# Output projection of the first block by seven products between attention pieces, with its operand sums made in parts

## The chip, the cores and the metric

The kernel runs on one core of one Trainium2 chip. The metric is the device time of one execution in microseconds (us), the median of three runs. In the profile the engines are called PE (matmuls), PEld (the weight loads of PE), DVE (vector engine), ACT (scalar engine), POOL and SP (the last two mainly issue transfers here). "Tile" names such as hT, wO or xT are those of the program's buffers.

## The reference, cut to what matters

Attention whose keys and values are first projected from 1024 positions to 64, then a gated feed-forward layer:

```python
k_proj = einsum('ks,bhsd->bhkd', E, k); v_proj = einsum('ks,bhsd->bhkd', F, v)
attn   = softmax(q @ k_proj.T / 8)                 # 8 batches, 8 heads, 1024 x 64
x      = (attn @ v_proj) as [8192 tokens, 512]
gate   = 1 / (1 + exp(-(x @ w_gate)))              # w_gate, w_val: 512 x 1536
val    = x @ w_val
out    = (gate * val) @ w_out                      # w_out: 1536 x 512
```

The kernel handles the tokens in 16 blocks of 512, two for each batch. For most of the matrix products it uses a scheme with seven products of half-sized operands in place of eight (the operands are split 2 by 2, and sums of the parts, called S for the left and T for the right operand, take part in the products). Before the change the first block is the exception: its gate, its values and its output projection are plain products.

## The kernel before

Each engine runs its instructions in the order in which the program adds them. The first stage (attention of batch 0, block 0, block 1, and attention of batch 1) is ordered by hand: a list `todo` of slots, and for each slot functions that are put behind it. The rest is ordered by a small list scheduler, `arranged`.

```python
todo.append(lambda: first_pair(0, lambda: xo(1)))          # slot 0: hidden parts m = 0, 1
for m in range(2, NF):                                      # slots 1..10: m = 2..11
    todo.append(lambda m=m: mstep(0, m))
put(3, lambda: (qt2(0, ("DVE", "ACT")), qt2(1, ("DVE", "ACT"))))
put(4, lambda: (sc2(0), sc2(1)))
put(4, second_loads)
put(6, lambda: (den2(), xo2(0), xo2(1)))
put(7, lambda: (vt_sums(3, 0), vt_sums(2, 0)))              # DVE, 0.42 us each
put(8, lambda: bc2(0)())                                    # PE, then 2 DVE multiplications into xT
put(9, lambda: bc2(1)())                                    # the same for the other half of xT
put(10, x_sums(1, 1, 2)); put(10, lambda: vt_sums(1, 0))
# ... slots 11..38: block 1, three rounds of nine: gate steps and seven value products
def on(u, j, fn): put(11 + 9 * u + j, fn)
on(3, 0, n1["mixed"])                                       # slot 38
on(3, 0, lambda: [late1(x, g) for x in ("A0", "A1") for g in range(2)])
on(3, 0, h_sums(1, Z, 1, 2, 3))                             # DVE sums of block 1's hidden part
for tt in range(4):                                         # slots 39..42
    todo.append(lambda tt=tt: oproj(0, tt, FF.take()))
on(3, 1, n1["outputs"])
on(3, 2, lambda: n1["bc"](0))
on(3, 3, lambda: n1["bc"](1))
```

A step of the gated layer of block 0 makes two banks (gate and value, 4 matmuls of 512 columns each) and joins them; the DVE instruction of `gate` frees the value bank. There are four such banks.

```python
def mstep(blk, m):
    pbs = {n: ffn.next() for n in "GV"}
    for n in "GV":
        for i in range(NI):
            mm_one(blk, m, i, n, pbs[n])        # reads xT[:, i, block], all four i
    gate(blk, m, pbs["G"], pbs["V"])            # ACT tanh, DVE (tanh + 1) * value -> hT
```

The output projection of block 0, four times 12 matmuls of 512 columns, each with one DVE instruction that halves the sum on its way out of the bank:

```python
def oproj(blk, tt, pb, cols=((0, DM),)):
    ...
    for m in range(NF):
        mm(pb, bank[pb][:, 0 : c1 - c0], hT[blk % 2][:, m, tt * P : (tt + 1) * P], wO[:, m, c0:c1], ...)
    dve(lambda e: e.tensor_scalar(o[:, c0:c1], bank[pb][:, 0 : c1 - c0], 0.5, None, op0=ALU.mult), ...)
    FF.append(pb)
    add("SP", lambda e: e.dma_start(out_v[blk // 2, t][:, c0:c1], o[:, c0:c1]), ...)
```

The attention pieces of batch 1 that stand between them (`mixed`, `outputs`, `bc`). The banks FF (four) and AA (four) are handed on in the order in which the program gives them back:

```python
def mixed3():                                   # slot 38
    f, a0, a1 = FF.two(), AA.two(), AA.two()
    sc_one(3, f); xo_one(0, a0); xo_one(1, a1)  # PE
    for g in range(2): exp_half(3, g, f); FF.append(f[g])      # ACT
    later("A0", x_half, 0, a0, AA); later("A1", x_half, 1, a1, AA)   # ACT copies, give the banks back
def outputs3():                                 # slot 39
    f, a0 = FF.two(), AA.two()
    bd = AA.take()                              # the third AA bank to come back
    den8(bd); xo_one(2, f); xo_one(3, a0)       # PE: 16, 4 and 4 matmuls
    for g in range(2): x_half(2, g, f); ...     # ACT copies
    for g in range(2): x_half(3, g, a0); ...
    rec(0); rec(1)                              # DVE reciprocals of the denominators
    split()                                     # DVE: rden -> rhi, rhl (two instructions)
def bc(rnd):                                    # 8 matmuls that read rhl, into all four AA banks,
    ...                                         # then 4 DVE multiplications into xT
```

The sums of w_out (`t_sums`, four DVE instructions of 1536 elements a row) and of the weights of the gate (`gt_sums`, likewise) are made at the start of the scheduled stage; the former overwrite the place where bsel8, rhi and rhl lie:

```python
plan.tasks = []
...
next_kv, t_sums (3, 2), gt_sums (3, 2, 4, 1), xs_sums, t_sums (4, 1)
o_chain(1, ...)       # seven products for block 1's output projection
...
for t in arranged(tasks, {"DVE": 1.5}):         # when DVE is taken to be free, us after the stage's start
    ...
```

The weights of gate and value come in pieces of 256 columns, in the order of `m`:

```python
load_w(0, 0); load_w(0, 1); load_w(1); load_w(2)
for R in range(2): load_q_half(0, 1, R)
load_w(3); load_w(4); load_w(5)
```

Of the kernel before, what the change touches and what calls it, by code (L numbers as in the profile page):

```python
# [7 lines left out]
ALU = mybir.AluOpType  # L8
# [229 lines left out]
def bass_linformer_attn__then__ffn_glu_sigmoid_kernel(  # L238
# [18 lines left out]
    with contextlib.ExitStack() as es:  # L257
# [30 lines left out]
        identf = within([P, P], FP32)  # L288
        bsel8f = within([P, 4, 2, 64], FP32)
        early[0], used[0] = wT[:, :, :, :].rearrange("p a b c -> p (a b c)"), 0  # L290
        bsel8 = within([P, 4, 2, 64], BF16)
        kp = within([P, NR, DH], BF16)
        rhi = within([P, 256], BF16)
        rhl = within([P, 256], BF16)
        early[0], used[0] = gT[:, :, :, :].rearrange("p a b c -> p (a b c)"), 0
        rden = within([P, 256], FP32)
        rows = within([P, 4, 32], FP32)
# [93 lines left out]
        def dve(fn, r, w, b=None, t=None):  # L391
            x = [] if b is None else [("bank", b)]
            return add("DVE", fn, r=r, w=w, x=x, t=t)
# [78 lines left out]
        def start_loads():  # L472
            for src, rows, n in ((E, slice(0, 64), "E"), (F, slice(64, 128), "F")):
                add(
                    "SP",
                    lambda e, src=src, rows=rows: e.dma_start(EF[rows, :], src[:, :]),
                    w=[("EF", n)],
                    dma="in" + n,
                )
            for i in range(4):  # L480
                pool(
                    lambda e, i=i: e.memset(quad[32 * i : 32 * i + 32, :], 32.0 * i),  # L482
                    w=[("quad", i)],
                )
            for R in range(2):
                load_kv_heads(0, k, R)
                load_q_half(0, 0, R)
            for R in range(2):
                load_kv_heads(1, v, R)
            load_w(0, 0)  # L490
            load_w(0, 1)
            load_w(1)
            load_w(2)
            for R in range(2):
                load_q_half(0, 1, R)
            load_w(3)
            load_w(4)
            load_w(5)

        def heads8():  # L500
# [781 lines left out]
        def mm_one(blk, m, i, n, pb):  # L1282
# [8 lines left out]
                stop=(i == NI - 1),  # L1291
            )

        def gate(blk, m, pg, pv):
            M = blk * NF + m
            sg = sig[M % 3]
            act(
                sg, bank[pg][:, :], [], [("sig", M % 3, 0)], b=pg, func=AF.Tanh, scale=0.5
            )
            dve(  # L1300
                lambda e: e.scalar_tensor_tensor(
                    hT[blk % 2][:, m, :],
                    sg,
                    1.0,
                    bank[pv][:, :],
                    ALU.add,
                    ALU.mult,
                ),
                [("sig", M % 3, 0)],
                [("hT", blk % 2, m, n) for n in range(2)],  # L1310
                b=pv,
            )

        def oproj(blk, tt, pb, cols=((0, DM),)):
            o = vsnap[tt][:, :] if tt < 2 else ost[:, tt, :]
            ok = [("vsnap", tt)] if tt < 2 else None
            t = 2 * (2 * (blk % 2) + tt % 2) + tt // 2
            for n, (c0, c1) in enumerate(cols):
                if n:
                    pb = FF.take()  # L1320
                for m in range(NF):
                    mm(
                        pb,
                        bank[pb][:, 0 : c1 - c0],
                        hT[blk % 2][:, m, tt * P : (tt + 1) * P],
                        wO[:, m, c0:c1],
                        [("hT", blk % 2, m, tt // 2)] + (["wO0", "wO12"] if m < H6 else ["wO1"]),
                        start=(m == 0),
                        stop=(m == NF - 1),
                    )  # L1330
                dve(
                    lambda e, pb=pb, c0=c0, c1=c1: e.tensor_scalar(
                        o[:, c0:c1], bank[pb][:, 0 : c1 - c0], 0.5, None, op0=ALU.mult
                    ),
                    [],
                    ok or [("ost", tt, x) for x in ((0, 1) if len(cols) == 1 else (n,))],
                    b=pb,
                )
                FF.append(pb)
                add(  # L1340
                    "SP",
                    lambda e, c0=c0, c1=c1: e.dma_start(out_v[blk // 2, t][:, c0:c1], o[:, c0:c1]),
                    r=ok or [("ost", tt, x) for x in ((0, 1) if len(cols) == 1 else (n,))],
                    dma=f"out{tt}" if n == 0 else "outlast",
                )

        H6 = NF // 2

        def t_sums(n):
            B11, B12 = wO[:, 0:H6, 0:256], wO[:, 0:H6, 256:512]
            B21, B22 = wO[:, H6:NF, 0:256], wO[:, H6:NF, 256:512]
            T4, T3, T2 = [wT[:, i, :, :] for i in range(3)]
            o, a, b, op, r, w = {
                3: (T3, B22, B12, ALU.subtract, ["wO1", "wO12"], [("wT", 3)]),
                2: (T2, T3, B11, ALU.add, ["wO0", ("wT", 3)], [("wT", 2)]),
                4: (T4, B21, T2, ALU.subtract, ["wO1", ("wT", 2)], [("wT", 4)]),  # L1360
                1: (B12, B12, B11, ALU.subtract, ["wO0"], ["wO12", ("wT", 1)]),
            }[n]
            if n == 4:
                w = w + ["bsel8", ("kp", 0), ("kp", 1)]
                w += [(k, R) for k in ("rhi", "rhl") for R in range(2)]
            dve(lambda e: e.tensor_tensor(o, a, b, op), r, w, t=0.95)

        def s_sums(blk, n, ms, eng="DVE"):
            h, (m0, m1) = hT[blk % 2], ms
            lo, hi, up = slice(m0, m1), slice(H6 + m0, H6 + m1), range(m0, m1)  # L1370
            A11, A21 = h[:, lo, 0:256], h[:, lo, 256:512]
            A12, A22 = h[:, hi, 0:256], h[:, hi, 256:512]
            S1, S2 = hS[:, 0, lo, :], hS[:, 1, lo, :]
            o, a, b, op, r, w = {
                1: (S1, A21, A22, ALU.add, "A21 A22", "S1"),
                2: (S2, S1, A11, ALU.subtract, "S1 A11", "S2"),
                3: (A21, A11, A21, ALU.subtract, "A11 A21", "A21"),
                4: (A12, A12, S2, ALU.subtract, "A12 S2", "A12"),
            }[n]
            add(  # L1380
                eng,
                lambda e: e.tensor_tensor(o, a, b, op),  # L1382
                r=[k for x in r.split() for k in part(blk, x, up)],
                w=part(blk, w, up),
                t=0.95 if m1 - m0 == 6 else 0.6,
            )

        def part(blk, x, up):
            if x[0] == "S":
                return [(x, m) for m in up]  # L1390
            return [("hT", blk % 2, m + H6 * (x[2] == "2"), int(x[1]) - 1) for m in up]

        def product(blk, bk, A, B, start=False, stop=False, js=(0, 1), ms=(0, NF // 2), also=()):
            h = hT[blk % 2]
            for j in js:
                for m in range(*ms):
                    if A[0] == "S":
                        lhsT = hS[:, int(A[1]) - 1, m, j * P : (j + 1) * P]
                    else:
                        c = 256 * (A[1] == "2") + j * P  # L1400
                        lhsT = h[:, m + H6 * (A[2] == "2"), c : c + P]
# [61 lines left out]
        def evac(bk, tok, col):  # L1463
            o, keys = quarter(tok, col)
            act(o, bank[bk][:, :].rearrange("p (j c) -> p j c", j=2), [], keys, b=bk, scale=0.5)

        def o_chain(blk, a, c, goal, step, sums=True):
            turn = [0]
# [123 lines left out]
        def gt_sums(n, part=None):  # L1592
# [14 lines left out]
            w = [("gT", n, j) for j in js]  # L1607
            if n != 1:
                w += ["rows", "ident"] + [("rden", c, R) for c in range(2) for R in range(2)]
            if n == 1:  # L1610
                r, w = [("wG", j, 0) for j in js], w + [("wG", 3 + j, 0) for j in js]
            if n == 2:
# [324 lines left out]

        A, Z = (0, 4), (4, 6)
        todo.append(lambda: first_pair(0, lambda: xo(1)))
        for m in range(2, NF):  # L1940
            todo.append(lambda m=m: mstep(0, m))
        qt2, sc2, den2, bc2, xo2 = half_unit(1, att)
        put(3, lambda: (qt2(0, ("DVE", "ACT")), qt2(1, ("DVE", "ACT"))))
# [36 lines left out]
        def on(u, j, fn):  # L1980
            put(11 + 9 * u + j, fn)
# [21 lines left out]
        on(2, 0, h_sums(1, A, 1))  # L2003
        on(2, 4, h_sums(1, A, 2, 3))
        on(3, 0, h_sums(1, Z, 1, 2, 3))
        for tt in range(4):
            todo.append(lambda tt=tt: oproj(0, tt, FF.take()))
        on(3, 1, n1["outputs"])
        on(3, 2, lambda: n1["bc"](0))
        on(3, 3, lambda: n1["bc"](1))  # L2010

        for i, slot in enumerate(todo):
            slot()
# [19 lines left out]
            vd_one(XA, 0, b % 2)  # L2033
            vd_one(XA, 1, b % 2, b > 3)

        for n in (3, 2):
            t_sums(n)
        for n in (3, 2, 4):
            gt_sums(n)
        gt_sums(1)  # L2040
# [1 line left out]
            xs_sums(2, n)  # L2042
        next_kv(2, -2.0)
        transpose_q(["kpB"])
        t_sums(4)
        t_sums(1)
        o_chain(1, OA, OC, 0.0, 2.0, sums=False)
        for n in (1, 2, 3, 4):
            xs_sums(3, n)
# [43 lines left out]
                    xs_sums(2 * b + 3, i)  # L2093

        tasks, plan.tasks = plan.tasks, None
        for t in arranged(tasks, {"DVE": 1.5}):
            for eng, fn, r, w, x, dma in t.calls:
                add(eng, fn, r=r, w=w, x=x, dma=dma)

# [28 lines left out]
```

The softmax here doesn't subtract the row's maximum and nothing guards it: scores larger than these inputs give would overflow.

## Time and profile before

| | |
|---|---|
| median of 3 runs | 517.51 us (516.99 to 517.76) |
| span of the profiled execution | 515.9 us |
| PE busy | 505.0 us (98%) |
| DVE busy | 410.9 us (80%) |
| ACT busy | 345.0 us (67%) |
| granted PE clock | 1.000 |

How to read it: the two numbers of a line in the timeline are the start, in us from the start of the span, and the length; a line joins several instructions of one kind, and the idle time of the engine ahead of them stands in brackets with what ended it. Matmuls are pipelined, so that the end of a matmul is later than the start of the next; the distance of two starts is what a matmul costs PE. In the table by stretches each engine has its busy time, and in brackets the number of its instructions.

### The profile page before, as it was taken

How to read it: one execution, taken by the hardware profiler on the slowest of the kernel's cores; microseconds unless marked ns; L12 is line 12 of the kernel's file. 1: busy time of each engine (PE TensorE's matmuls, PEld its weight loads, DVE VectorE, ACT ScalarE, POOL GpSimd, SP SyncE). 2: the span in 40 equal slices, each digit the busy share in tenths (PEclk: the TensorE clock that was granted, in tenths of full speed). 3: DMA queues.
4: the chain of work that ended last, by engine and by line, in shares of the span. 5: the costliest groups of instructions: out<-in, count | busy, mean ns of one | idle time of the engine just before them, and what ended most of it. 6: DMA issues, size and time to landing. Idle time of an engine off the chain costs nothing.

```text
span 515.9 us, 11369 instructions
## 1 busy us (share of the span) xinstructions
PE 505.0 (98%) x4598; PEld 410.0 (79%) x4598; DVE 410.9 (80%) x809; ACT 345.0 (67%) x645; POOL 41.0 (8%) x60
## 2 busy tenths in 40 slices
PE   5999999999999999999999999999999999999996
PEld 3545645888888888888888888888888888888885
DVE  4548779899789796988879888797969898777774
ACT  2555683867778677677767776777676766676652
POOL 9420301200200020000100020000000000000000
PEclk9999999999999999999999999999999999999999
DMA  9999999899798788454946389374104330201013
GB/s 161 199 198 204 150 195 221 115 178 233 93 224 155 152 150 138 102 125 123 174 85 154 60 152 203 56 164 100 46 7 97 42 104 1 83 1 76 6 43 124
DMA packets 105205, 63.13 MB, mean 122 GB/s; under 512 B 63040, under 2 KB 97344, under 8 KB 105152
## 3 DMA queue, kind: packets, MB, share of 16 engines
q0 software_dynamic: 34000, 29.89, 37.5%
q1 hardware_dynamic: 71152, 32.52, 28.8%
q8 instruction: 36, 0.59, 0.4%
q14 instruction: 17, 0.14, 0.1%
HBM read 60.29 MB, written 16.78 MB: 149 GB/s over the span
## 4 chain that ended last, share of the span: by engine, by line
PE 94%; DMA 2%; DVE 1%; POOL 1%; issue 0%; ACT 0%; DVEq 0%; POOLq 0%
PE pA L385 51%; PE pF L385 43%; DMA KVs<-in_v_dram 2%; DVE hT L1832 0%; POOL KVs L403 0%; DVE vsnap L1710 0%; POOL Qb L403 0%; DVE xT L868 0%; DVE ost L1437 0%; ACT sig L389 0%; DVE sig L1786 0%; ACT vsnap L389 0%; DVE ost L1522 0%; POOL quad L482 0%; DVE hS L1382 0%
## 5 line engine op out<-in xcount | busy, mean ns | idle before, releaser
L389 ACT ACTIVATE sig<-pA 128x512 f32<-128x512 f32 x126 | 75.1, 596 | 43.4 <-PE pA L385 42.8
L1699 ACT ACTIVATE pF<-pA 128x512 f32<-128x512 f32 x99 | 58.5, 591 | 30.9 <-PE pA L385 26.3
L1710 DVE TENSOR_TENSOR vsnap<-pF,vsnap 128x512 f32<-128x512 f32 x90 | 61.8, 686 | 18.1 <-ACT vsnap L389 9.2
L1786 DVE TENSOR_TENSOR sig<-pF,sig 128x512 f32<-128x512 f32 x84 | 57.5, 685 | 7.2 <-PE pA L385 3.7
L385 PE MATMUL pF<-wO,hT 128*128 128x256 bf16 (+1 forms) x402 | 59.3, 285 | 0.0
L389 ACT ACTIVATE vsnap<-pA 128x512 f32<-128x512 f32 x84 | 50.2, 597 | 11.9 <-PE pA L385 11.8
L1832 DVE SCALAR_TENSOR_TENSOR hT<-sig,vsnap 128x512 bf16<-128x512 f32 x84 | 56.6, 683 | 0.9
L389 ACT ACTIVATE sig<-sig 128x512 f32<-128x512 f32 x84 | 52.8, 629 | 2.9 <-DVE sig L1786 2.6
L385 PE MATMUL pF<-xS,wV 128*128 128x256 bf16 x360 | 54.0, 273 | 0.1
L385 PE MATMUL pA<-xT,gT 128*128 128x256 bf16 x336 | 50.4, 273 | 0.0
L385 PE MATMUL pF<-xS,wG 128*128 128x256 bf16 x336 | 50.4, 273 | 0.0
L385 PE MATMUL pA<-xT,vT 128*128 128x256 bf16 x336 | 50.4, 273 | 0.0
L385 PE MATMUL pF<-xT,wG 128*128 128x256 bf16 (+1 forms) x264 | 50.2, 311 | 0.2 <-DVE xT L868 0.2
L389 ACT ACTIVATE sig<-pF 128x512 f32<-128x512 f32 x66 | 39.5, 598 | 15.0 <-PE pF L385 13.1
L385 PE MATMUL pA<-wT,hT 128*128 128x256 bf16 x360 | 48.8, 273 | 0.1
L1832 DVE SCALAR_TENSOR_TENSOR hT<-sig,pF 128x512 bf16<-128x512 f32 x42 | 28.7, 683 | 24.6 <-PE pF L385 24.4
L385 PEld LDWEIGHTS pF<-wO,hT 128*128 128x128 bf16 x402 | 38.7, 98 | 10.5 <-issue 0.8
L385 PE MATMUL pF<-xT,wV 128*128 128x256 bf16 (+1 forms) x240 | 41.5, 294 | 0.0
L385 PEld LDWEIGHTS pF<-xS,wV 128*128 128x128 bf16 x360 | 34.9, 98 | 6.1 <-DVE vsnap L1710 0.4
L385 PEld LDWEIGHTS pA<-wT,hT 128*128 128x128 bf16 x360 | 34.3, 98 | 5.6 <-ACT EF L389 0.8
L389 ACT ACTIVATE eT<-pA 128x512 bf16<-128x512 f32 x58 | 34.1, 596 | 5.7 <-PE pA L385 4.4
L385 PEld LDWEIGHTS pA<-xT,vT 128*128 128x128 bf16 x336 | 32.3, 98 | 5.2 <-issue 0.4
(159 smaller groups left out, 906.5 us busy)
## 6 DMA issues: line engine op xcount, KB each, us to landing
out_dram<-ost SPq DMA_DIRECT2D x61, 256.0 KB, 2.5
Qb<-in_q_dram POOLq DMA_DIRECT2D x7, 1024.0 KB, 11.9
KVs<-in_k_dram POOLq DMA_DIRECT2D x7, 1024.0 KB, 13.7
KVs<-in_v_dram POOLq DMA_DIRECT2D x7, 1024.0 KB, 18.0
wO<-in_moe_w_out_dram POOLq DMA_DIRECT2D x2, 768.0 KB, 9.8
wG<-in_moe_w_gate_dram POOLq DMA_DIRECT2D x5, 256.0 KB, 18.9
wV<-in_moe_w_val_dram POOLq DMA_DIRECT2D x5, 256.0 KB, 19.4
KVs<-in_k_dram POOLq DMA_DIRECT2D x2, 512.0 KB, 9.3
```

What stands on the lines that cost most here:

```text
L385: return add("PE", lambda e: e.matmul(o, lhsT, rhs, **kw), r=r, x=[("bank", b)])
L389: return add("ACT", lambda e: e.activation(o, i, func, scale=scale), r=r, w=w, x=x, t=t)
L1699: lambda e: e.activation(bank[c][:, :], bank[a][:, :], AF.Copy, scale=1.0),
L1710: lambda e: e.tensor_tensor(o, bank[bk][:, :], o, ALU.add),
L1786: dve(lambda e: e.tensor_tensor(o, bank[bk][:, :], o, ALU.add), [key], [key], b=bk)
L1832: lambda e: e.scalar_tensor_tensor(o, sg.rearrange("p (j c) -> p j c", j=2), 1.0, x.rearrange("p (j c) -> p j c", j=2), ALU.add, ALU.mult,),
```

## The change

The output projection of the first block is to be made with the seven products too (84 matmuls of 256 columns in place of 48 of 512). They stand as pieces between the attention pieces of batch 1. For this, four things move:

- The sums of block 0's hidden part (S) are made in three parts of two `m` and one last sum, as soon as the hidden parts of which they consist are there. S1 and S2 lie in the buffer of the gate's sums, gT, which is not filled until later.
- So that a part has its two halves (`m` and `m + 6`) early, the steps of block 0 run in the order 0, 1, 6, 7, 2, 3, 8, 9, 4, 5, 10, 11, and the weight pieces load in that order.
- The sums of w_out are made ahead of the products, in the first stage, and no longer in the scheduled one; bsel8, rhi and rhl have buffers of their own for it.
- The scheduler takes DVE to be free after 2.5 us and not 1.5.

```diff
-        bsel8 = within([P, 4, 2, 64], BF16)
-        rhi = within([P, 256], BF16)
-        rhl = within([P, 256], BF16)
+        bsel8 = sbuf("bsel8", [P, 4, 2, 64], BF16)
+        rhi = sbuf("rhi", [P, 256], BF16)
+        rhl = sbuf("rhl", [P, 256], BF16)
...
             load_w(0, 1)
+            load_w(3)
             load_w(1)
-            load_w(2)
             for R in range(2):
                 load_q_half(0, 1, R)
-            load_w(3)
             load_w(4)
+            load_w(2)
             load_w(5)
...  (oproj is taken out; gate counts its own turns for its buffers)
+        def o_pieces(blk):
+            a, c = FF.two()
...
+            return [
+                do(p(a, "A11", "B11", True), lambda: seed(a, c)),
+                do(p(c, "A12", "B21"), lambda: evac(c, 0, 0)),
+                do(p(a, "S2", "T2"), lambda: keep_snap(0, a)),
+                p(c, "S1", "T1", True),
+                do(p(a, "A21", "T3"), lambda: keep_snap(1, a), lambda: add_snap(1, c, 1, 1)),
+                do(p(a, "A22", "T4"), lambda: evac(a, 1, 0), lambda: stored(blk, (2, 3))),
+                do(p(c, "A12", "B22"), lambda: add_snap(0, c, 0, 1), lambda: stored(blk, (0, 1))),
+                lambda: (FF.append(a), FF.append(c)),
+            ]
...
-        for m in range(2, NF):
+        for m in (6, 7, 2, 3, 8, 9, 4, 5, 10, 11):
             todo.append(lambda m=m: mstep(0, m))
...
-        for tt in range(4):
-            todo.append(lambda tt=tt: oproj(0, tt, FF.take()))
+        o0 = []
+        todo.append(lambda: (o0.extend(o_pieces(0)), o0[0]()))
+        todo.extend([lambda n=n: o0[n]() for n in range(1, 8)])
+        on(3, 0, lambda: [t_sums(n) for n in (3, 2, 1)])
         on(3, 1, n1["outputs"])
-        on(3, 2, lambda: n1["bc"](0))
-        on(3, 3, lambda: n1["bc"](1))
+        on(3, 1, lambda: t_sums(4))
+        on(3, 3, lambda: n1["bc"](0))
+        on(3, 5, lambda: n1["bc"](1))
+        put(3, h_sums(0, (0, 2), 1, 2))
+        put(4, h_sums(0, (0, 2), 3))
+        put(7, h_sums(0, (2, 4), 1, 2))
+        put(8, h_sums(0, (2, 4), 3))
+        on(1, 8, h_sums(0, (4, 6), 1, 2, 3))
+        on(3, 4, h_sums(0, (0, 6), 4))
...
-        for n in (3, 2):
-            t_sums(n)
...
-        t_sums(4)
-        t_sums(1)
...
-        for t in arranged(tasks, {"DVE": 1.5}):
+        for t in arranged(tasks, {"DVE": 2.5}):
```

In `o_pieces`, `seed` (ACT) copies bank a into bank c, so that the next product can add to it; `evac` and `keep_snap` (ACT) take a halved bank out; `add_snap` (DVE) adds a bank to what was kept.

## The prediction

> **What bounds the kernel now.** I read the page's busy times first, then the table by stretches, then the timelines of PE, DVE and ACT around the places that the change touches.
>
> ```profile
> PE 505.0 (98%) x4598; PEld 410.0 (79%) x4598; DVE 410.9 (80%) x809; ACT 345.0 (67%) x645; POOL 41.0 (8%) x60
> ```
>
> PE is busy for 98% of the span. That share is an average, so the stretches come next: the one with the four projections of block 0, and the long steady part.
>
> ```profile
> core 0: us, PE busy (x) PEld busy (x) DVE busy (x) ACT busy (x) POOL busy (x), PEclk, DMA share, GB/s
> 70.70:83.50 12.80, 12.80 (x92) 5.17 (x90) 11.53 (x20) 4.75 (x10) 0.00 (x0) 1.00 1.22 224
> 150.00:500.00 350.00, 350.00 (x3237) 304.60 (x3236) 290.89 (x559) 248.13 (x464) 7.90 (x9) 1.00 0.48 98
> ```
>
> In both PE never stops: what is saved on PE shortens the run, and what stops PE early in the run is never made up later, because the steady part has no idle PE to absorb it. In the first of the two DVE is busy too, 11.53 of 12.80 us, and ACT is not.
>
> PE's timeline shows the places (start, length):
>
> ```profile
> 45.75 0.81 PE L385 MATMUL pF<-xT,wV 128*128 128x512 bf16 x3
> 46.40 1.03 PE L385 MATMUL pF<-xT,wG 128*128 128x512 bf16 x4
> ...
> 70.74 2.76 PE L385 MATMUL pF<-wO,hT 128*128 128x512 bf16 x12
> 73.44 0.62 PE L385 MATMUL pA<-eT,dsel 128*32 128x256 bf16 x16
> ...
> 77.24 0.40 PE L385 MATMUL pA<-wT 32*128 32x256 bf16 x8
> 77.57 2.76 PE L385 MATMUL pF<-wO,hT 128*128 128x512 bf16 x12
> ...
> 83.50 1.92 PE L385 MATMUL pA<-KVs,EFT 128*64 128x512 bf16 x16
> 93.23 0.82 PE L385 MATMUL pA<-wT,hS 128*128 128x256 bf16 x6
> 93.88 0.60 PE L385 MATMUL pF<-xS,wG 128*128 128x256 bf16 x4
> ```
>
> Projections and attention pieces take turns from 70.74 to 83.50, where the scheduled stage begins. Beside it DVE (three places) and ACT:
>
> ```profile
> 42.38 0.42 DVE L1590 TENSOR_TENSOR vT<-vT,wV 128x512 bf16<-128x512 bf16 x1
> 42.72 0.68 DVE L1301 SCALAR_TENSOR_TENSOR hT<-sig,pF 128x512 bf16<-128x512 f32 x1
> ...
> 45.11 1.28 DVE L833 TENSOR_TENSOR xT<-pA,xu 128x512 bf16<-128x512 f32 x2
> ```
>
> ```profile
> 72.55 0.42 DVE L1382 TENSOR_TENSOR hT<-hT 128x512 bf16<-128x512 bf16 x1
> ...
> 74.27 1.77 DVE L1004 RECIPROCAL gT<-pA 128x128 f32<-128x128 f32 x2
> ...
> 76.40 0.48 DVE L1034 SCALAR_TENSOR_TENSOR wT<-wT,gT 128x256 bf16<-128x256 bf16 x1
> ...
> 84.21 0.95 DVE L1617 TENSOR_TENSOR gT<-wG 128x1536 bf16<-128x1536 bf16 x1
> ```
>
> ```profile
> 64.44 0.60 ACT L1699 ACTIVATE pF<-pF 128x512 f32<-128x512 f32 x1
> ...
> 71.31 2.08 ACT L389 ACTIVATE xu<-pA 128x512 f32<-128x512 f32 x4
> ```
>
> The reader is to see two tight hand-overs: the multiplication into xT that ends at 46.39, just as PE starts on that xT at 46.40; and the last step of rhl, done at 76.88, 0.36 us before the piece that reads it, at 77.24.
>
> **What the Trainium skill says.** *TensorE: Matmul & The Clock Gate*, "Wait — 56ns, not 53.3ns?", gives a warm matmul as columns over 2.4 GHz plus about 2.5 ns. The trace agrees: starts lie 216 ns apart for 512 columns and 109 for 256 (six in 93.88 - 93.23 = 0.65 us). So a matmul of half the columns costs half, and seven products save PE time. *TensorEngine Tiling (Array Packing)*, "Key Properties": changing the tiling mode drains the engine. Here 12 matmuls of 216 ns make 2.60 us, but 73.44 - 70.74 is 2.70: about 0.1 us for a change of form. The pieces between the projections stay four, and so do the changes. *TensorE*, "Architectural detail: the array is 16× 32×32, not 1× 128×128": ACT and DVE are strict first in, first out. The timelines show no exception, and my reckoning rests on it: where a sum is put in DVE's program matters more than how long it takes.
>
> **The change part by part.**
>
> *Matmuls.* Removed: 48 x 0.217 = 10.4 us. Added: 7 products x 12 x 0.1092 = 9.2 us. PE gains 1.24 us.
>
> *Sums of block 0, first part* (slots 3 and 4). Three DVE instructions of 512 elements, 0.42 us each. DVE sits idle before the next steps there for over a microsecond (1.27 and 2.26 us in its timeline). No cost.
>
> *Second part* (slots 7 and 8). S1 and S2 come right behind the vT sum of 42.38, and S3 behind the first multiplications. From 41.32 to 46.4 DVE has no gap, so it slips: the value step of 42.72 by 0.78 us (two sums at spacing 0.45 and 0.33), the second pair of multiplications by 1.15 (one more at 0.35). That pair then ends at 47.54 in place of 46.39. PE's gate step of 46.40 reads two quarters of xT that are there and then, from 46.83, the two that are not: PE waits some 0.75 us. Afterwards DVE is no later relative to PE than it was.
>
> *Third part* (slot 28, about 63 us). Three sums, 1.2 us, stand ahead of the addition to vsnap that DVE starts at 63.07. It ends at 64.87 and not 63.76; the ACT copy of 64.44 writes that bank and slips to about 64.93; the product of 65.10 needs it and slips to 65.55. PE waits 0.45 us.
>
> *The stage from 70.74.* Each engine in its order:
> - PE's first product (12 x 0.109 = 1.31 us) ends at 72.05, where the whole projection lasted to 73.44. The denominators then want the third AA bank, which the third of the four ACT copies (71.31 on, 0.48 apart) gives back at 72.89. PE waits 0.8 us, then 1.11 us of attention to 74.06. The seed copy follows the fourth ACT copy, 73.3 to 73.9, so it is in time. Two products take PE to 76.68.
> - DVE ends the last hidden sum at 72.97 and now does three sums of w_out (0.95 us each, spaced 0.98, 0.87 and 0.87 as one needs another's result) ahead of the reciprocals, where it had 0.58 us idle and a 0.69 us eviction. So the reciprocals start at 75.62 in place of 74.27, and rhl is ready at 78.23 in place of 76.88.
> - `bc(0)` therefore runs at 78.3, while PE has been free from about 76.8: a wait of 1.5 us. It is the largest new one.
> - Two products (2.6 us) follow to 81.25. DVE's fourth w_out sum precedes its four multiplications (0.6 us apart), which end and free the banks for `bc(1)` at 81.5: 0.2 us. Then `bc(1)` (0.33) and two products, to 84.6.
>
> So the scheduled stage starts at 84.6 instead of 83.50, 1.1 us later, with the 1.24 us saved already in it. The five ACT copies and two DVE additions of the new projection (0.60 and 0.69 us, against four DVE evictions) fit beside this.
>
> *The scheduled stage.* It loses the four w_out sums, 3.7 us of DVE. PE idles for 0.16, 0.20 and 0.04 us there before, at 88.6, 91.4 and 92.8; perhaps 0.3 of it goes. DVE gets to it about 1.7 us behind PE (it was 0.7), which fits the scheduler's new 2.5 for 1.5. The gate's sums have 4 to 5 us until PE wants them, so I expect no new wait.
>
> *Loads.* The pieces have the same sizes and land in the same places of the order, and the steps use them in that order: nothing.
>
> Sum: 0.75 + 0.45 + 1.1 - 0.3 = +2.0 us, 519.5. I take 519.0, a little lower, since each wait comes from short hand-overs of which one may turn out milder than I count.
>
> **The rivals.** (1) *The sums hide and PE keeps its gain*: 517.5 - 1.24 - 0.3, about 516.0. For it: PE bounds, DVE is idle 20% of the span, and the pieces look placed with care, in parts and early. Against it: the two hand-overs shown, with 0.01 and 0.36 us to spare. (2) *Only the late stage costs*: the early sums slip in, 517.5 + 1.1 - 0.3 = 518.3. For it: the early places have a little idle DVE (0.27 us at 46.7, 0.98 at 66). Against it: all of that lies behind the point where PE waits. (3) *A pile-up*: DVE enters the scheduled stage so late that the first seven-product chains of the gate wait as well, or ACT's strict order (seed, copies and evictions in one queue) stops products too. Each such wait is of the order of one instruction, 0.6 to 0.95 us, which makes 520 to 521.5. Against it: the chains of block 1's output projection are there as filler without DVE.
>
> **Range and chances.** The floor is the first rival, the ceiling the third. I put 0.7 on slower than before at all, and a range of 516.0 to 521.0 for eight times in ten. Nothing here comes near 2% (10.4 us): within 2% 0.98, faster 0.005, slower 0.015.
>
> **What would show it.** In the profile after: PE's new matmuls at 0.109 us apart, 84 of them; a PE wait of about 0.75 us on DVE's xT near 46.8; one of about 0.45 near 65; one of about 0.8 on ACT ahead of the denominators; one of about 1.5 on DVE's rhl ahead of `bc(0)`; the scheduled stage's first KVs product about 2.3 us later than 83.50. I am wrong if that product starts before 83.5, or if DVE runs in another order than the program's. The weak steps are the places of the second and third part of the sums, and that nothing after 90 us gives time back.

## The result, and the profile after

The changed kernel takes 521.03 us (median of 6 runs, 519.88 to 521.60) against 517.50 (median of 6 runs): the ratio is 1.0063, with a 95% interval of 1.0046 to 1.0079. The change made the kernel slower, by 3.5 us of the two medians; the prediction was 519.0, with a range of 516.0 to 521.0. The span of the profiled execution went from 515.9 to 519.2 us.

The first part of the page after, and the same kind of stretches, now for the stretch from the first product to the start of the scheduled stage:

```profile
PE 504.1 (97%) x4634; PEld 413.2 (80%) x4634; DVE 414.2 (80%) x817; ACT 348.7 (67%) x650; POOL 41.0 (8%) x60
```

```profile
72.30:86.40 14.10, 11.78 (x126) 8.70 (x124) 13.93 (x23) 7.52 (x15) 0.00 (x0) 1.00 1.07 178
150.00:500.00 350.00, 350.00 (x3237) 304.50 (x3236) 291.72 (x564) 247.84 (x463) 7.90 (x9) 1.00 0.47 98
```

PE's busy time did go down, by 0.9 us, and the run became longer all the same. In the stretch of the projection PE has idle time now (11.78 of 14.10 us), and it is DVE that is busy throughout (13.93 of 14.10). The bound has changed hands there. The steady part is as full as before.

PE's timeline after (start, length, and in brackets the idle time ahead of a line with what ended it):

```profile
46.80 0.59 PE L385 MATMUL pF<-xT,wG 128*128 128x512 bf16 x2
47.98 0.60 PE L385 MATMUL pF<-xT,wG 128*128 128x512 bf16 x2 [0.58 <-DVE xT L833]
...
66.69 0.61 PE L385 MATMUL pF<-xT,wV 128*128 128x256 bf16 x4 [0.33 <-ACT pF L1690]
...
72.33 1.48 PE L385 MATMUL pF<-wO,hT 128*128 128x256 bf16 x12
74.54 0.62 PE L385 MATMUL pA<-eT,dsel 128*32 128x256 bf16 x16 [0.72 <-ACT xu L389]
...
76.97 1.47 PE L385 MATMUL pF<-wT,gT 128*128 128x256 bf16 x12
79.87 0.40 PE L385 MATMUL pA<-rhl,bsel 32*128 32x256 bf16 x8 [1.43 <-DVE rhl L1034]
80.20 1.48 PE L385 MATMUL pF<-wO,gT 128*128 128x256 bf16 x12
...
82.93 0.59 PE L385 MATMUL pA<-rhl,bsel 32*128 32x256 bf16 x8
83.68 1.49 PE L385 MATMUL pF<-wT,hT 128*128 128x256 bf16 x12 [0.17 <-ACT EF L389]
...
86.41 1.92 PE L385 MATMUL pA<-KVs,EFT 128*64 128x512 bf16 x16
...
90.45 0.60 PE L385 MATMUL pF<-xT,wG 128*128 128x256 bf16 x4
91.48 0.83 PE L385 MATMUL pF<-wO,hT 128*128 128x256 bf16 x6 [0.43 <-ACT pF L1690]
92.15 0.60 PE L385 MATMUL pA<-xS,gT 128*128 128x256 bf16 x4
```

A gate step is cut in two at 46.80, an ACT copy comes late at 66.69, the denominators wait at 74.54, and the piece that reads rhl waits at 79.87: the four waits that the prediction named, each at its place. Two more it did not name: at 83.68 and at 91.48 PE waits for ACT copies. The idle time in brackets is a little shorter than what a wait costs, because the end of a matmul is modelled: by the distance of starts, with a matmul's own cost taken off, the four named places cost 0.75, 0.49, 0.89 and 1.59 us, with 0.1 in the third and fourth for the change of form that stood there before too, and the one at 91.48 costs 0.59.

DVE's timeline of the same stretch shows why rhl is late:

```profile
74.14 0.42 DVE L1352 TENSOR_TENSOR hT<-hT 128x512 bf16<-128x512 bf16 x1
74.47 0.95 DVE L1331 TENSOR_TENSOR wT<-wO 128x1536 bf16<-128x1536 bf16 x1
75.46 0.96 DVE L1331 TENSOR_TENSOR wT<-wT,wO 128x1536 bf16<-128x1536 bf16 x1
76.34 0.95 DVE L1331 TENSOR_TENSOR wO<-wO 128x1536 bf16<-128x1536 bf16 x1
77.21 1.76 DVE L1004 RECIPROCAL gT<-pA 128x128 f32<-128x128 f32 x2
...
79.33 0.48 DVE L1034 SCALAR_TENSOR_TENSOR rhl<-rhi,gT 128x256 bf16<-128x256 bf16 x1
```

The three sums of w_out lie between the last hidden sum and the reciprocals, without a gap. Before, 1.72 us passed from the start of that hidden sum to the reciprocals (72.55 to 74.27); now 3.07.

To compare executions I use three distances of PE's timeline, which leave out how early the first transfers landed: from the first gate product to the first KVs product of the scheduled stage (A), from there to the second next group of KVs products, at 172.09 before (B), and the rest (C). A scatters by some 0.2 us (62.14 before, 61.90 in the run whose steps only stand in another order). C is 343.75 to 343.78 us in all the profiles for which A and B are given here. So whatever happens before is carried to the end, to a few hundredths of a us.

| profile | A | B | C |
|---|---|---|---|
| before | 62.14 | 88.59 | 343.76 |
| after | 65.48 | 88.99 | 343.78 |

A is 3.34 us longer, 0.83 of it a wait on the second half of q near 31 us that no other profile has at this length; B is 0.40 longer. That execution reached its first gate product 0.43 us sooner, and 3.34 + 0.40 + 0.02 - 0.43 = 3.3 is the difference of the spans.

### The profile page after: what moved, and what is told of

Same layout as the page of the kernel before. It is cut to its first block, busy times and chain, and to the rows that moved or that the text cites. A ratio compares the mean times of both kernels' runs of the same rounds, so it can differ in the third digit from the quotient of the medians.

```text
span 519.2 us, 11454 instructions
## 1 busy us (share of the span) xinstructions
PE 504.1 (97%) x4634; PEld 413.2 (80%) x4634; DVE 414.2 (80%) x817; ACT 348.7 (67%) x650; POOL 41.0 (8%) x60
## 4 chain that ended last, share of the span: by engine, by line
PE 88%; DMA 4%; DVE 3%; POOL 2%; ACT 1%; issue 1%; ACTq 0%; DVEq 0%; POOLq 0%
PE pA L385 49%; PE pF L385 39%; DMA Qb<-in_q_dram 4%; POOL KVs L403 1%; DVE vsnap L1701 1%; POOL wG L403 1%; POOL wV L403 1%; DVE hT L1674 0%; POOL Qb L403 0%; DVE hT L1823 0%; DVE wT L1331 0%; ACT pF L1690 0%; DVE gT L1004 0%; ACT kpd L389 0%; DVE wO L1331 0%
## 5 line engine op out<-in xcount | busy, mean ns | idle before, releaser
L385 PE MATMUL pF<-wO,hT 128*128 128x256 bf16 x390 | 52.7, 273 | 0.4 <-ACT pF L1690 0.4
L385 PEld LDWEIGHTS pF<-wO,hT 128*128 128x128 bf16 x390 | 37.6, 98 | 6.1 <-ACT pF L1690 0.7
L385 PEld LDWEIGHTS pA<-xT,gT 128*128 128x128 bf16 x336 | 31.3, 98 | 6.4 <-issue 0.8
```

The costliest lines, as they stand in the source:

```text
L385: return add("PE", lambda e: e.matmul(o, lhsT, rhs, **kw), r=r, x=[("bank", b)])
```

## The experiments

All times are medians, the ratio is to the kernel before, measured beside it on the same chip.

| run | us | ratio, 95% interval | A | B |
|---|---|---|---|---|
| order of loads and steps alone | 517.54 | 1.0001 (0.9992 to 1.0009) | 61.90 | 88.59 |
| second and third part moved | 519.52 | 1.0041 (1.0027 to 1.0055) | 63.22 | 89.21 |
| w_out sums left out of the stretch | 519.51 | 1.0037 (1.0025 to 1.0048) | 62.92 | 89.71 |
| scheduler's 1.5 | 520.63 | 1.0058 (1.0045 to 1.0071) | 64.42 | 88.53 |
| ACT's order alone | 521.46 | 1.0081 (1.0064 to 1.0097) | 65.09 | 89.00 |
| all by order, on DVE | 519.40 | 1.0037 (1.0025 to 1.0049) | 63.90 | 88.53 |
| the same, bank first | 518.49 | 1.0021 (1.0014 to 1.0028) | 63.22 | 88.53 |
| products without sums | 516.90 | 0.9983 (0.9976 to 0.9990) | 61.47 | 88.59 |
| w_out sums on POOL | 530.10 | 1.0237 (1.0215 to 1.0258) | | |
| w_out loaded early | 523.59 | 1.0120 (1.0107 to 1.0133) | | |

### The order of the loads alone

```diff
 (the kernel before)
-load_w(0, 1); load_w(1); load_w(2); q halves; load_w(3); load_w(4); load_w(5)
+load_w(0, 1); load_w(3); load_w(1); q halves; load_w(4); load_w(2); load_w(5)
-for m in range(2, NF):
+for m in (6, 7, 2, 3, 8, 9, 4, 5, 10, 11):
```

> The kernel before with the new order of the weight pieces and of the steps of block 0, and nothing else of the change. Theory (order of the loads costs nothing; the 0.7 us for which PE waited on the second half of q in the changed kernel's profile is a matter of that one execution): 517.5 us within 0.3, and no wait on q above 0.3 us in the profile. Rival (the new order of the pieces delays that half of q): 518.1 to 518.4, with the wait on q again in the profile at 31 us.

Measured: 517.54 us, ratio 1.0001, no wait on q. The order costs nothing and brings nothing. The wait on q in the changed kernel's profile is no lasting cost of this order: the runs below that keep the order have none, or 0.2 us.

### The second and third part of the hidden sums in an idle place

```diff
-put(7, h_sums(0, (2, 4), 1, 2)); put(8, h_sums(0, (2, 4), 3))
-on(1, 8, h_sums(0, (4, 6), 1, 2, 3))
+on(1, 3, h_sums(0, (2, 4), 1, 2, 3)); on(1, 3, h_sums(0, (4, 6), 1, 2, 3))
```

> The changed kernel, with the second and third part of the sums of block 0's hidden part moved to where DVE sits idle (behind the hidden step of round 1, some 58 to 61 us). Theory (these sums cost PE time because they stand ahead of DVE steps for which PE waits): the waits of 0.75 us at 47 and 0.45 us at 66 are gone, the time falls by 1.2 us to 519.8. Rival (DVE has too much to do in all, and the wait comes back elsewhere before the projection): 520.7 to 521.3.

Measured: 519.52 us, and the waits at 47 and 66 us are gone from PE's timeline. By the medians that is 1.5 us, and by distance A 63.22 against 65.48 - 0.83 = 64.65, 1.4 us. B is 0.2 us longer, and the cause of that stays open; A and B together give 1.2 us, which is what the two waits made (0.75 + 0.49). The six sums are the same, on the same engine; what they cost was their place.

### No w_out sums in that stretch

```diff
-on(3, 0, lambda: [t_sums(n) for n in (3, 2, 1)]); on(3, 1, lambda: t_sums(4))
+(the four sums again at the start of the scheduled stage)
 def product(...):
+    if blk == 0 and B in ("T2", "T3", "T4"): rhs, k = wO[:, m, 0:256], "wO0"
+    (and T1 waits for nothing but wO)
```

> The changed kernel, with the four sums of w_out back in the scheduled stage; the products of block 0 read pieces of w_out itself where they would read the sums, so the first block's output is left without its proper operands: all the work of the products, without the sums ahead of them. Theory (these sums, 3.7 us of DVE ahead of the reciprocals and multiplications, make the 1.4 us wait on rhl and the later ones up to the scheduled stage): the wait ahead of bc(0) falls under 0.2 us, the scheduled stage starts 1.5 to 2.2 us earlier, time 518.8 to 519.5. Rival (the stage is held by ACT's copies and the banks that they give back): no more than 0.5 us, 520.5 or more.

Measured: 519.51 us. PE's timeline of this run:

```profile
76.36 1.47 PE L385 MATMUL pF<-wO,gT 128*128 128x256 bf16 x12
77.77 0.40 PE L385 MATMUL pA<-rhl,bsel 32*128 32x256 bf16 x8
...
84.31 1.92 PE L385 MATMUL pA<-KVs,EFT 128*64 128x512 bf16 x16
```

The piece that reads rhl follows its product at once. From the start of the first product (71.73 here, 72.33 in the changed kernel) to the KVs product it is 12.58 us in place of 14.08: 1.5 us, at the low end of what was expected. Part of it is given back: B is 89.71, 0.7 us longer than in the changed kernel, with the sums back in the scheduled stage and its 2.5 kept.

### The scheduler's 1.5 us

```diff
-for t in arranged(tasks, {"DVE": 2.5}):
+for t in arranged(tasks, {"DVE": 1.5}):
```

> The changed kernel, with the scheduler's 1.5 us in place of 2.5. Theory (the 0.6 us wait of PE on ACT's seed copy at 91 us comes of the order that 2.5 makes: both of block 1's second products drawn ahead): 0.4 to 0.6 us less, 520.5. Rival (DVE is late at that point, and 1.5 makes PE wait on the sums of the gate instead): 521.0 to 522.

Measured: 520.63 us; the interval overlaps that of the changed kernel, so the time alone does not tell them apart. The trace does: the wait of 0.59 us at 91 us is not there, and B is 88.53 in place of 88.99. PE's timeline of this run:

```profile
91.10 0.60 PE L385 MATMUL pF<-xT,wG 128*128 128x256 bf16 x4
91.54 0.60 PE L385 MATMUL pA<-xS,gT 128*128 128x256 bf16 x4
92.13 0.83 PE L385 MATMUL pF<-wO,hT 128*128 128x256 bf16 x6
```

With 2.5 (the lines of 90.45 to 92.15 above), the scheduler puts the second product of block 1's projection right behind the gate's, ahead of a product of the gate that needs a sum from DVE; the product that it draws ahead then stands waiting for its ACT seed copy.

### ACT's order alone

```diff
 o_pieces:  A11 B11, A12 B21, S2 T2,
-           S1 T1, A21 T3, ...
+           A21 T3, S1 T1, ...
-f, a0 = FF.two(), AA.two(); bd = AA.take()
+f, bd = FF.two(), AA.take(); a0 = AA.two()
+(the last of the four attention copies behind the seed copy)
```

> The changed kernel with only ACT's side in another order: the seed copy ahead of the last attention copy, the denominators' bank taken first, A21 T3 ahead of S1 T1. Theory (in that stretch DVE is full from the sums of w_out on, and sets when rhl is ready): the wait of 0.9 us ahead of the denominators shrinks to under 0.3, the wait ahead of bc(0) grows by what was saved there to about 2.2 us, and the time gains 0.2 to 0.5 us at most, from the 0.4 us copy wait after bc(1). Rival (each wait has its own cost): 0.8 to 1.3 us less, 519.8 to 520.2.

Measured: 521.46 us, no gain at all; A is 65.09, 0.4 us longer than the 64.65 above. PE's timeline of this run:

```profile
71.50 1.48 PE L385 MATMUL pF<-wO,hT 128*128 128x256 bf16 x12
72.92 0.62 PE L385 MATMUL pA<-eT,dsel 128*32 128x256 bf16 x16
...
79.04 0.40 PE L385 MATMUL pA<-rhl,bsel 32*128 32x256 bf16 x8 [1.91 <-DVE rhl L1034]
...
86.24 1.05 PE L385 MATMUL pA<-KVs,EFT 128*64 128x512 bf16 x8 [0.83 <-DVE xT L1087]
```

The wait ahead of the denominators is gone, and so is the copy wait behind the second `bc`; the one on rhl has grown by 0.5 us, and a new one of 1.0 us (by starts) stands ahead of the KVs product. For the wait ahead of the denominators the first of the two theories holds. From the first product to the piece that reads rhl it is 7.54 us here (71.50 to 79.04) and 7.54 us in the changed kernel (72.33 to 79.87): DVE sets that time, and PE's wait on ACT only filled a part of it. The gain that the theory expected from the copy behind the second `bc` did not come, because the new wait took it back. The new wait is of my edit's making: with the banks in another order, the one that the KVs product wants is given back by the last multiplication.

### The w_out sums on POOL

```diff
+put(6, h_sums(0, (2, 4), 1, 2, 3)); on(1, 3, h_sums(0, (4, 6), 1, 2, 3))
-dve(lambda e: e.tensor_tensor(o, a, b, op), r, w, t=0.95)     # t_sums
+pool(lambda e: e.tensor_tensor(o, a, b, op), r, w)
```

> The changed kernel, with the second part of the hidden sums right behind the step that makes rhl for block 0 (DVE idle 1.2 us there), the third in the gap at 58 to 61 us, and the four sums of w_out made by POOL, which has nothing else to do then, in place of DVE. Theory (the cost lay in what stands ahead of what in DVE's queue, not in the sums themselves): the waits at 47, at 66 and ahead of bc(0) are gone, 1.2 + 1.5 us and the run's own scatter, 518.0 to 518.6, if POOL needs 2 us or less for each sum. Rival (POOL is slow at this, or slows DVE while both work on the same memory): PE waits on wT instead, or DVE's instructions of that stretch grow longer, 519.5 to 522.

Measured: 530.10 us, 9 us slower than the changed kernel. My theory failed here, and the rival held in both of its halves, at a price far above the 519.5 to 522 that it named: PE waited 1.8 us for a sum in wT, and DVE's instructions grew longer. POOL's timeline, then DVE's:

```profile
71.55 3.09 POOL L1331 TENSOR_TENSOR wT<-wO 128x1536 bf16<-128x1536 bf16 x1 [7.89 <-DMA wO<-in_moe_w_out_dram]
74.72 3.42 POOL L1331 TENSOR_TENSOR wT<-wT,wO 128x1536 bf16<-128x1536 bf16 x1
```

```profile
72.03 3.17 DVE L1674 SCALAR_TENSOR_TENSOR hT<-sig,vsnap 128x512 bf16<-128x512 f32 x1
75.11 3.30 DVE L1352 TENSOR_TENSOR hS<-hT 128x512 bf16<-128x512 bf16 x1
78.45 3.19 DVE L1352 TENSOR_TENSOR hS<-hS,hT 128x512 bf16<-128x512 bf16 x1
```

A POOL sum takes 3.1 to 3.4 us where DVE needs 0.95. Worse, each of the four DVE instructions that began beside one lasted until 0.3 to 0.6 us after POOL's ended: sums of 0.42 us became 3.2 to 3.3. DVE did four instructions in 13 us, rhl was ready at 87.4 us in place of 79.8, and PE waited 7.8 us for it. The Trainium skill says this: *SBUF — State Buffer*, "Who interferes with whom", has a DVE instruction with two inputs in SBUF contend with a GpSimd instruction that reads SBUF, and one block the other wholly. The four that were stretched all have two inputs in SBUF, so the trace agrees. The place to look for free time was the memory port that both engines share, not POOL's empty queue.

Two more runs stood on this one and so tell little by themselves. ACT's order on top of it:

> As the run with POOL's sums, and ACT's side in another order: the seed copy ahead of the last of the four attention copies, the denominators' bank taken first and not third of those that come back, and the product A21 T3 ahead of S1 T1, so that each copy out of a bank has another product beside it. Theory (PE waits 0.9 us on the third attention copy and 0.4 us on the copy of A21 T3, because ACT does its copies in order): 0.8 to 1.2 us less than the run with POOL's sums, 517.0 to 517.6. Rival (the seed copy is the next bound, and PE waits for it instead): no more than 0.3 us less.

Measured: 529.59 us, ratio 1.0221 (1.0198 to 1.0244). This run's profile shows that not every DVE instruction is held up. While a POOL sum ran (first line), DVE made two reciprocals, whose one input is a bank, and then a cast, whose one input lies in SBUF:

```profile
77.20 3.26 POOL L1331 TENSOR_TENSOR wO<-wO 128x1536 bf16<-128x1536 bf16 x1
77.44 1.76 DVE L1004 RECIPROCAL gT<-pA 128x128 f32<-128x128 f32 x2
79.23 1.38 DVE L1032 CAST rhi<-gT 128x256 bf16<-128x256 f32 x1
```

The reciprocals took 1.76 us, as without POOL's sums; the cast took 1.38 in place of 0.29 and ended 0.15 us after POOL's sum. So what POOL stretched here was not only instructions with two inputs in SBUF.

And the scheduler's 1.5 on top of both:

> As the run with ACT's order, and the scheduler's 1.5 us in place of 2.5. Theory (with DVE relieved of the sums, it reaches the scheduled stage as early as in the kernel before, so 1.5 fits and the 0.6 us wait on a seed copy at about 90 us is gone): 516.5 to 517.1, which is under the kernel before by what the products save, 0.5 to 1 us. Rival (the wait only moves): no difference to the run before it.

Measured: 528.48 us, ratio 1.0212 (1.0198 to 1.0226). In the latter's profile PE still waits 7.8 us on rhl. Their questions were asked again on DVE, below.

### All that order can do, with the sums on DVE

The second part of the hidden sums at slot 6, the third in round 1, ACT's order and the scheduler's 1.5 as above, and:

```diff
-on(3, 0, lambda: [t_sums(n) for n in (3, 2, 1)]); on(3, 1, lambda: t_sums(4))
+on(3, 0, lambda: [t_sums(n) for n in (3, 2)]);    on(3, 1, lambda: [t_sums(n) for n in (1, 4)])
```

> The changed kernel with all that can be had by order alone: the second part of the hidden sums behind rhl of block 0, the third in the gap at 58 to 61 us, ACT's order as above, the sums T1 and T4 of w_out behind the reciprocals and rhl and not T1 ahead of them, and the scheduler's 1.5 us. All sums on DVE. Theory: minus 1.2 (parts), minus 0.4 (scheduler), minus 0.9 for rhl that is one sum earlier, and minus up to 0.4 for the copy wait: 518.2 to 518.8, still behind the kernel before, because T3 and T2 still stand ahead of rhl. Rival (order is all, the sums cost nothing by themselves): 516.5 to 517.3.

Measured: 519.40 us, more than either theory said. The wait ahead of `bc(0)` fell only to 1.2 us by starts, and the wait of 1.0 us ahead of the KVs product came along with ACT's order. So that was taken out next:

```diff
 def bc(rnd):
+    if rnd: AA.sort(key=lambda x: x != A3)      # the bank that the KVs product takes
```

> As the run with everything ordered on DVE, and the second bc takes first the bank that the scheduled stage's first product wants, so that DVE's first and not last multiplication gives it back. Theory (the 1.0 us wait ahead of that product in the two runs with the banks in another order came of this alone): the wait is under 0.2 us and the time 0.7 to 1.0 us less, 518.2 to 518.7. Rival (DVE is full up to there, and PE waits for it a little later instead): less than 0.4 us less, 519.0 or more.

Measured: 518.49 us. The KVs wait is gone and 0.9 us with it (0.7 by A). It is not all gain, though: the second `bc` now waits 1.2 us by starts for DVE's multiplications, about what its two waits made in the run before (1.1). This is the fastest complete version of the change that I ran, and it is still slower than the kernel before, by 0.14 to 0.28%.

### w_out loaded early

As "all by order, on DVE", with T3 and T2 in DVE's gaps of round 2, and the load that must land for it no longer held back:

```diff
 load(wO[...], moe_w_out..., f"wO{x}",
-     r=turned()[:2])           # behind the transposes of q
+     )
```

> As the run with everything ordered on DVE, and w_out's load does not wait for the transposes of q, so that it lands by some 64 us in place of 70.5, and T3 and T2 are made in DVE's gaps at 65 and 69 us. Theory (T3 and T2 ahead of rhl are the rest of the cost, and DVE has about 1.6 us of gap there): 516.6 to 517.4, level with the kernel before or a little under it, and the wait ahead of bc(0) is under 0.3 us. Rival (the earlier w_out transfer pushes back the values of batch 1, which land at 56.4, or the transposes): PE waits on KVs or qT between 52 and 64 us, 518 or more.

Measured: 523.59 us; the rival holds. The wait ahead of `bc(0)` is gone, as the theory wanted. But the four transposes of q landed at 54.9 to 67.5 us, against 56.2 to 59.6 in the changed kernel, and PE waited for them:

```profile
66.75 0.64 PE L385 MATMUL pF<-qT,kpD 64*64 64x512 bf16 x4 [4.88 <-DMA qT<-Qb]
...
69.00 1.91 PE L385 MATMUL pF<-xT,wG 128*128 128x512 bf16 x4
```

The condition on that load, which looks like a lost chance in the kernel, keeps the DMA engines free for the transposes.

### The products without their sums

```diff
 product(...):
+    if A[0] == "S" and blk == 0: A = {"S1": "A21", "S2": "A11"}[A]
+    (w_out's pieces in place of T, as above)
-(all h_sums of block 0; t_sums again in the scheduled stage)
```

with ACT's order, the bank order and the scheduler's 1.5.

> All 84 products and their copies for the first block, but none of the sums that they need: no S sums of block 0 (its products read hidden parts themselves in their place), the w_out sums left in the scheduled stage and replaced by pieces of w_out, so that the first block's output lacks its proper operands. ACT's order, the bank order and the scheduler's 1.5 us as in the run beside it. Theory (the products save 1.24 us of PE, and it is the sums in DVE's queue that cost more than that): 516.0 to 516.8, under the kernel before. Rival (seven products between attention pieces lose by themselves, through the copies between their banks): 517.5 or more.

Measured: 516.90 us, ratio 0.9983 (0.9976 to 0.9990): 0.1 us above what the theory said, and under the kernel before. The first block's output lacks its proper operands, so this is no version to use; it shows what the products are worth by themselves. PE's timeline:

```profile
70.69 1.48 PE L385 MATMUL pF<-wO,hT 128*128 128x256 bf16 x12
...
77.00 2.79 PE L385 MATMUL pF<-wO,hT 128*128 128x256 bf16 x24 [0.41 <-ACT EF L389]
...
82.78 1.92 PE L385 MATMUL pA<-KVs,EFT 128*64 128x512 bf16 x16
```

From the first product to the KVs product it is 12.09 us, against 12.76 for the four plain projections. Of the 1.24 us that PE saves, 0.57 is lost to copies between the banks, above all the one ahead of the line of 77.00. So with the copies in this order the most that the change could bring, in this stretch, was about 0.7 us, and that only if DVE's sums cost nothing.

## Why the prediction was right, and where it fell short

The direction, the mechanism and the places were right. The time, 521.03, lies 0.03 us above the upper end of the range: what was mis-sized was so in one direction. The half microsecond that I took off my sum of 519.5, because a wait might turn out milder, found no support: none was milder. The steps, one by one:

- *PE saves 1.24 us by the products*: right. Twelve of them take 1.31 us from start to start (75.65 to 76.97: 1.32), as reckoned, and the run without sums came out under the kernel before.
- *First part of the hidden sums, no cost*: right; no wait there.
- *Second part, 0.75 us at 46.8; third part, 0.45 at 65*: right in place and size (0.75 and 0.49 by starts), and shown by moving the sums alone, which took both away.
- *The denominators wait 0.8 us for an ACT copy, `bc(0)` 1.5 us for rhl*: measured 0.89 and 1.59. That the second is due to the w_out sums is shown by leaving them out. The two are not to be added up: I took `bc(0)` at 78.3 us from DVE's path alone, 7.56 us behind the first product, and the run with ACT's order alone shows that path to be the one that counts, 7.54 us with the first wait and without it.
- *The stage from 70.74 ends 1.1 us later*: it was 1.32 (14.08 - 12.76). The term that was short is the ACT copy behind `bc(1)`. I had PE wait 0.2 us for DVE ahead of that piece and then go on. It lost that 0.2 us inside the piece, and then 0.2 more on A21 T3's copy, which ACT could start only when that product was done: from 82.93 to 83.68 it is 0.75 us, where the piece of `bc(0)` took 0.33.
- *The scheduled stage gives 0.3 us back*: wrong. It took 0.40 more (B). I reasoned that DVE has less to do there, and that block 1's products fill in; I did not ask what the scheduler's new 2.5 does to the order. It drew one such product ahead of its ACT seed copy, and the run with 1.5 shows that this made the 0.40. But even with 1.5 B is 88.53, only 0.06 us less than before: without the four w_out sums on DVE there, the stage gave practically nothing back either way.
- *Loads, nothing*: right, by the run with the order alone.

Added up as the profile has them, 0.75 + 0.49 + 1.32 + 0.40 is 3.0 us where the prediction had 2.0. The rest of the 3.5 us I can't assign. In the two runs with 22 executions each, the medians and the distances agree better: bank first is 1.06 us behind the kernel before by the medians and 1.02 by A and B, products without sums 0.53 and 0.67 ahead of it. That points to scatter in a median of six. The first gate product of the profiles lies between 20.3 and 22.7 us, so that how the first transfers land moves one execution by more than that rest, and the six runs of the changed kernel are 1.7 us apart; but it was not settled which part of the medians' difference that is.

Of the rivals, the first (the sums hide) fell, and so did the second (only the late stage costs), with the two early waits. The third (a pile-up at the scheduled stage) was nearest in time. What came of it was the wait on an ACT copy at 91.48, and that was made by the scheduler's order; the profile shows no chain of the gate that waited for DVE's sums there.

## What to carry to other kernels

When one engine is full, look at what the work taken from it lays on the next: here 1.24 us of matmuls were bought with 4.7 us of new vector sums, and 3.8 us of others were brought forward into a stretch where the vector engine had 1.3 us to spare. Where engines run in order, place decides: the same six sums cost 1.2 us or nothing. A wait that you remove on one engine brings nothing where another engine sets the time of the same point. An idle engine or an idle DMA queue is not free capacity until you know what it shares with the busy ones.

## What the runs showed of the hardware that I had not expected

PE's granted clock fell to half after waits of several microseconds, which made long waits cost more than their length. The table by stretches of the run with w_out loaded early (PE's clock is the number ahead of the last two):

```profile
61.70:66.70 5.00, 0.17 (x2) 0.00 (x0) 2.79 (x5) 0.36 (x1) 0.00 (x0) 0.76 1.39 144
66.70:70.70 4.00, 3.95 (x20) 1.63 (x21) 0.36 (x1) 2.17 (x4) 2.49 (x3) 0.50 0.35 26
```

After the wait of 4.88 us the four gate matmuls of 69.00 took 1.71 us to the next line's start, where 0.86 is usual. The run with POOL's sums shows it too, after its 7.8 us (12 matmuls from 87.99 to 90.53, nearly twice their time). The two runs on top of it show how long a wait that takes (first the run with ACT's order, then the one with 1.5 too):

```profile
77.29 2.74 PE L385 MATMUL pF<-wT,gT 128*128 128x256 bf16 x12 [3.52 <-POOL wT L1331]
76.80 1.50 PE L385 MATMUL pF<-wT,gT 128*128 128x256 bf16 x12 [2.01 <-POOL wT L1331]
```

A wait of 3.52 us was enough to slow the matmuls behind it, and one of 2.01 us was not. The Trainium skill, *TensorE: Matmul & The Clock Gate*, "HAM oscillation — how this bites in real kernels", tells of this for idle gaps above some 3.4 us, which fits. The waits of the changed kernel behind its first gate product, 1.6 us at most, left the clock at 1.00.
